# Agent attention with a routed two-layer net: float32 second layer in the last ten token tiles of three batches

## The chip, the core and the metric

The kernel runs on one core of a Trainium2 chip. The metric is the time of one execution on the device in microseconds (us). Smaller is better. Times here are the median of the runs shown, and the profile is one further execution taken by the hardware profiler.

## What is computed

The reference does agent attention (4 batches of 11456 tokens with 128 channels, 49 agents) and sends each of the 45824 resulting rows through one of 8 experts, chosen by the largest cosine logit:

```python
a2k = sm(agents, k)          # softmax over tokens
agent_v = a2k @ v            # 49 x 128
q2a = sm(q, agents)          # softmax over the 49 agents
x = q2a @ agent_v
...
h = np.maximum(x[mask] @ w1[e], 0.0)       # 128 -> 1024
out[mask] = gate_w[mask, None] * (h @ w2[e])  # 1024 -> 128
```

## The kernel before, in words

Almost all tokens of a batch go to one expert, so the kernel picks that expert per batch (`pick_expert`, from line 610) and repairs the few other tokens at the end (`fix`, `stray`). It doesn't multiply all 1024 hidden units: `pick_expert` ranks them, keeps the first 256 (384 in the fourth batch) as real relu units, and treats the rest as always on or always off. The always-on ones are folded into one linear product with `lin`; `proved` (from line 975) checks every token against that assumption (tile `vp`). The first layer is folded with the attention values, so its input is the tile `tt` of softmax numerators, transposed.

One batch is 23 token tiles `t`: 22 tiles of 4 columns of 128 tokens and a last one of 2 columns of 96 tokens. Each tile runs through two 128-unit slices `f` (three in the fourth batch). For one (batch, tile, slice), called a step here:

- `ffn_mm1` (line 1121): TensorE makes `hp` (128 units by 512 tokens, float32 in PSUM) with two float16 products (lines 1129, 1130, weights split into a high part `gh` and a low part `gl`). ScalarE writes relu(hp) as float16 `hh` (line 1133). VectorE writes the float16 remainder `hl` = relu(hp) - hh (line 1134).
- `ffn_mm2` (line 1137), five ticks later (`LAG = 5`): for each column of 128 tokens, three float16 products into `yp`: hh with the high part of w2, hh with its low part, hl with the high part (lines 1157 to 1159). At the first slice of a tile the `lin` products go ahead of them (line 1148).
- `ffn_out` (line 1163): VectorE multiplies `yp` by the gate into `ot` (line 1173), and ScalarE's queue sends it to HBM.

PSUM has four banks for `hp`, the transposes `fTp` and the check `vp`, two for `yp` and two for all else. `hh` and `hl` have five buffers each, `ot` three.

Beside the steps of batch b run the key, value and query work of the coming batches (scores `sp`, transposes `fTp`, copies `fT`, value sums `avp`) and, near the end of batch b, `pick_expert` for batch b+1: mostly small VectorE steps one after another (`key`, `nkey`, `sel`, `rank`) with a few TensorE products (`gp`, `row`, `placed`, `linp`, `w2pp`). At its end the next batch's `gh`, `gl` and `w2p` exist, and its steps can begin.

The order of SyncE's queue is written out by the program. On the other engines the instructions are put in order when the kernel is built, by priorities (`ffn_mm1` has a raised one) and by the framework's own estimate of durations; `issue_after` pins a few of them behind others. Each engine then works off its queue in that order.

Of the kernel before, what the change touches and what calls it, by code (L numbers as in the profile page):

```python
# [8 lines left out]
F16 = mybir.dt.float16  # L9
BF16 = mybir.dt.bfloat16  # L10
F32 = mybir.dt.float32
F32R = mybir.dt.float32r
I32 = mybir.dt.int32
AF = mybir.ActivationFunctionType
ALU = mybir.AluOpType
# [3 lines left out]
P = 128  # L19
# [10 lines left out]
def kernel(ctx: ExitStack, tc: tile.TileContext, q, k, v, agents, emb, tau, w1, w2, out):  # L30
    nc = tc.nc
    pe, dve, act, pool, sp = nc.tensor, nc.vector, nc.scalar, nc.gpsimd, nc.sync

    B, N, C = q.shape
    A = agents.shape[1]
    E, D, F = w1.shape
# [4 lines left out]
    TICKS = 4  # L41
    AT = {2: {0: 0, 2: 1}, 3: {0: 0, 1: 1, 3: 2}}
    KEEP = 5

    REM_J, REM_P = 2, 96
    J = (N - REM_J * REM_P) // P
    TJ = 4
# [29 lines left out]
    cst = ctx.enter_context(tc.tile_pool(name="cst", bufs=1))  # L77
    ld = ctx.enter_context(tc.tile_pool(name="ld", bufs=LB))
    wk = ctx.enter_context(tc.tile_pool(name="wk", bufs=2))
    sm = ctx.enter_context(tc.tile_pool(name="sm", bufs=2))  # L80
# [8 lines left out]
    def psh(name):  # L89
        return ps_h.tile([P, 512], F32, name=name, tag="h")  # L90

    def psy(name):
        return ps_y.tile([P, 512], F32, name=name, tag="y")
# [16 lines left out]
    def give(o, i):  # L110
        o.left[i] -= 1
# [24 lines left out]
    def tshape(t):  # L136
        return (P, TJ) if t < NT - 1 else (REM_P, REM_J)

    def unit_of(t):
        return (t // UT, t % UT) if t < NT - 1 else (NU - 1, 0)  # L140
# [27 lines left out]
    unit_load(k, "k", 0, 0)  # L168
    unit_load(k, "k", 0, 1)
    ident = cst.tile([P, P], F32, name="ident")  # L170
    zeros = cst.tile([P, 512], F16, name="zeros")
    turned = []
    pool.memset(zeros, 0.0)

# [197 lines left out]
    y_last, h_last, p_last, q_last = [], [], [], []  # L372
# [637 lines left out]
    def mark_strays(b):  # L1010
# [37 lines left out]
        if b < B - 1:  # L1048
# [8 lines left out]
            yield 1  # L1057
            dve.tensor_scalar(had[:, :KEEP], top[:, :KEEP], 0.0, 0.0, ALU.is_gt, ALU.add, accum_out=cnt)
            yield 1
# [6 lines left out]
            yield 1  # L1066
            dve.tensor_scalar(had[:, :KEEP], iotaf[:, :KEEP], cnt, None, ALU.add)
            yield 1
            last = sm.tile([P, 1], F32, name="had2", tag="had2", bufs=1)
            dve.tensor_scalar(last, cnt, P - KEEP + 0.5, BIG, ALU.is_gt, ALU.mult)  # L1070
            yield 1
            dve.tensor_tensor(out=last, in0=last, in1=top[:, KEEP - 1 : KEEP], op=ALU.add)
            pick = sm.tile([P, KEEP, 2], F32, name="mpick", tag="mpick", bufs=1)
            dve.tensor_copy(pick[:, :, 0], top[:, :KEEP])
            yield 1
# [42 lines left out]
    ticks = [(b, t, r) for b in range(B) for t in range(NT) for r in range(TICKS)]  # L1118
    live, yps = {}, {}

    def ffn_mm1(b, t, f):
        bt = batches[b]
        u, w = unit_of(t)
        p, n = tshape(t)
        m = p * n
        tt = tts[b, u][:, w * TJ * P : w * TJ * P + m]
        hp = psh("hp")
        fs = slice(f * P, (f + 1) * P)
        pe.matmul(out=hp[:, :m], lhsT=bt.gh[:, fs], rhs=tt, start=True, stop=False)  # L1129
        pe.matmul(out=hp[:, :m], lhsT=bt.gl[:, fs], rhs=tt, start=False, stop=True)  # L1130
        hh = wk.tile([P, TJ * P], F16, name="hh", tag="hh", bufs=5)
        hl = wk.tile([P, TJ * P], F16, name="hl", tag="hl", bufs=5)
        h_last[:] = [act.activation(hh[:, :m], hp[:, :m], AF.Relu)]  # L1133
        dve.scalar_tensor_tensor(out=hl[:, :m], in0=hp[:, :m], scalar=0.0, in1=hh[:, :m], op0=ALU.max, op1=ALU.subtract)  # L1134
        live[b, t, f] = (hh, hl)

    def ffn_mm2(b, t, f):

        bt = batches[b]
        p, n = tshape(t)  # L1140
        hh, hl = live.pop((b, t, f))
        if f == 0:
            yp = yps[b, t] = psy("yp").rearrange("p (c d) -> p c d", d=D)
            u, w = unit_of(t)
            for c in range(n):
                tc_ = tts[b, u][:, (w * TJ + c) * p : (w * TJ + c + 1) * p]
                for h in range(2):
                    pe.matmul(out=yp[:p, c, :], lhsT=tc_, rhs=bt.lin[:, h], start=(c == 0 and h == 0), stop=False, skip_group_check=True)  # L1148
            give(t_slots, tt_of[b, u])
        yp = yps[b, t]  # L1150

        for c in range(n):
            y = yp[:p, c, :]
            cs = slice(c * p, (c + 1) * p)
            last = f == NMS[b] - 1 and c == n - 1
            wh, wl = bt.w2p[:, f, 0], bt.w2p[:, f, 1]
            pe.matmul(out=y, lhsT=hh[:, cs], rhs=wh, start=False, stop=False, skip_group_check=True)  # L1157
            pe.matmul(out=y, lhsT=hh[:, cs], rhs=wl, start=False, stop=False, skip_group_check=True)  # L1158
            y_last[:] = [pe.matmul(out=y, lhsT=hl[:, cs], rhs=wh, start=False, stop=last, skip_group_check=True)]  # L1159
        y_log.append((now[0], y_last[0]))  # L1160
# [377 lines left out]
    def step2(b, t, f):  # L1538
        ffn_mm2(b, t, f)
        if f == NMS[b] - 1:  # L1540
            spawn(ffn_out(b, t))
# [14 lines left out]
    with tc.manual_schedule(engines={mybir.EngineType.SP}):  # L1556
        due = []
        for i in range(len(ticks) + LAG):
            if i < len(ticks):
                b, t, r = ticks[i]  # L1560
                f = AT[NMS[b]].get(r)
                while f is not None and not (hasattr(batches[b], "gl") and (b, unit_of(t)[0]) in tts):
                    prove()
                    run_step()
                run_half()
                if f is not None:
                    with tc.high_priority(200):
                        ffn_mm1(b, t, f)
                    ffn_t[0] = (b, t)
                    due.append((i + LAG, b, t, f))  # L1570
            else:
                run_half()
            while due and due[0][0] <= i:
                _, b, t, f = due.pop(0)
                while not hasattr(batches[b], "w2p"):
                    run_step()
                step2(b, t, f)
            for _ in range(1 if len(jobs) < 12 and i < (B - 1) * S else 2):
                if i % 3 < 2 or len(jobs) > 6 or i >= (B - 1) * S:
                    prove()  # L1580
            run_half()
# [48 lines left out]
```

## Time and profile before

| | |
|---|---|
| median of 3 runs | 765.32 us (762.32 to 768.18) |
| profiled execution | 766.39 us, its span 764.6 us |
| TensorE (PE) busy | 692.7 us, 91% |
| its weight loads (PEld) | 570.6 us, 75% |
| VectorE (DVE) busy | 600.1 us, 78% |
| ScalarE (ACT) busy | 474.2 us, 62% |
| GpSimd (POOL) busy | 341.3 us, 45% |
| mean granted TensorE clock | 0.946 of full speed |

Busy time is the union of an engine's instructions. The ends of matmuls are modelled and overlap the next ones, so what a stream of matmuls costs is read from the distances of their starts. The chain of waits follows the work that ended last backwards through whatever released each step; its shares say where time would come off the end if a piece went away and nothing else took its place.

### The profile page before, as it was taken

The numbers are of one execution on the slowest core, as the hardware profiler recorded it, in microseconds if no ns is written. First come the engines' busy times: TensorE is split into PE (matmuls) and PEld (weight loads), VectorE is DVE, ScalarE is ACT, GpSimd is POOL, SyncE is SP. The second block draws the span as 40 slices with busy tenths as digits, with TensorE's granted clock in tenths as the row PEclk, the third lists the DMA queues.
The fourth block names the chain that finished last, engine by engine and source line by source line (L and its number), as shares of the span: only waits on it lengthen the run. The fifth ranks groups of instructions, "written<-read, shape, count | busy, mean of one in ns | idle before, by whom it ended". The sixth has DMA issues, their size and how long they took to land.

```text
span 764.6 us, 24029 instructions
## 1 busy us (share of the span) xinstructions
PE 692.7 (91%) x9644; PEld 570.6 (75%) x9644; DVE 600.1 (78%) x1556; ACT 474.2 (62%) x1161; POOL 341.3 (45%) x576
## 2 busy tenths in 40 slices
PE   8997989899869899999988889998996599999996
PEld 6886778778757687878876678887885386687675
DVE  5767887766479899958568989855778989779987
ACT  3436968576359477867467647754664347756763
POOL 5004402842424667565336435654536537254520
PEclk9988999999769999999997999999998899999999
DMA  9993269656397696698647259945352037414211
GB/s 330 283 345 136 90 160 247 148 165 187 74 326 208 124 202 194 174 234 199 213 125 189 69 149 241 245 127 159 99 169 82 21 88 176 102 46 112 68 47 63
DMA packets 157820, 122.62 MB, mean 160 GB/s; under 512 B 78728, under 2 KB 134106, under 8 KB 157708
## 3 DMA queue, kind: packets, MB, share of 16 engines
q1 hardware_dynamic: 144331, 97.44, 49.3%
q10 hardware_dynamic: 13120, 23.47, 9.6%
q8 instruction: 76, 1.25, 0.7%
q14 instruction: 37, 0.29, 0.1%
q0 software_dynamic: 256, 0.17, 0.1%
HBM read 79.14 MB, written 23.72 MB: 135 GB/s over the span
## 4 chain that ended last, share of the span: by engine, by line
PE 62%; DVE 19%; DMA 8%; ACT 4%; issue 3%; POOL 2%; SPq 1%; ACTq 0%; POOLq 0%; DVEq 0%
PE sp L429 8%; PE fTp L416 8%; PE avp L520 4%; PE yp L1157 4%; PE yp L1159 4%; PE hp L1129 4%; PE yp L1158 4%; PE yp L1148 4%; PE hp L1130 4%; DVE hl L1134 3%; PE vp L988 3%; DMA tt<-e 2%; DMA kt<-in_k_dram 2%; PE placed L735 2%; DVE sel L719 2%
## 5 line engine op out<-in xcount | busy, mean ns | idle before, releaser
L1134 DVE SCALAR_TENSOR_TENSOR hl<-hp,hh 128x512 f16<-128x512 f32 (+1 forms) x207 | 136.7, 666 | 38.2 <-ACT hh L1133 36.3
L1157 PE MATMUL yp<-w2p,hh 128*128 128x128 f16 (+1 forms) x810 | 155.8, 222 | 2.5 <-ACT hh L1133 2.5
L1133 ACT ACTIVATE hh<-hp 128x512 f16<-128x512 f32 (+1 forms) x207 | 119.3, 582 | 62.0 <-PE hp L1130 49.5
L1158 PE MATMUL yp<-w2p,hh 128*128 128x128 f16 (+1 forms) x810 | 155.8, 222 | 0.0
L1159 PE MATMUL yp<-w2p,hl 128*128 128x128 f16 (+1 forms) x810 | 152.5, 222 | 0.0
L997 ACT ACTIVATE vp<-vp 128x512 f32<-128x512 f32 x191 | 112.5, 589 | 33.6 <-PE vp L985 17.6
L429 PEld LDWEIGHTS sp<-aT_all,fT 128*64 128x64 f32 (+1 forms) x2400 | 86.4, 143 | 25.0 <-issue 12.8
L429 PE MATMUL sp<-aT_all,fT 128*64 128x49 f32 (+1 forms) x2400 | 100.5, 231 | 4.4 <-ACT av_all L596 1.8
L1157 PEld LDWEIGHTS <-hh 128*128 128x128 f16 (+1 forms) x810 | 81.5, 101 | 15.8 <-ACT hh L1133 3.7
L1159 PEld LDWEIGHTS <-hl 128*128 128x128 f16 (+1 forms) x810 | 81.3, 100 | 10.5 <-issue 1.1
L1158 PEld LDWEIGHTS <-hh 128*128 128x128 f16 (+1 forms) x810 | 81.1, 100 | 5.2 <-issue 0.2
L1129 PE MATMUL hp<-tt,gh 128*128 128x512 f16 (+1 forms) x207 | 77.7, 379 | 6.2 <-DVE hl L1134 2.0
L1130 PE MATMUL hp<-tt,gl 128*128 128x512 f16 (+1 forms) x207 | 77.6, 378 | 0.0
L1148 PE MATMUL yp<-lin,tt 128*128 128x128 f16 x720 | 63.6, 224 | 12.3 <-DVE ot L1173 10.4
L1173 DVE TENSOR_TENSOR ot<-yp,gs 128x512 f32<-128x512 f32 (+1 forms) x92 | 61.2, 669 | 16.7 <-PE yp L1159 9.4
L936 POOL TENSOR_TENSOR nrm<-qq,half 128x16 f32<-128x16 f32 (+2 forms) x28 | 69.1, 2469 | 0.3
L855 POOL TENSOR_TENSOR e<-qe,e 128x392 f16<-128x392 f32 (+1 forms) x44 | 39.8, 904 | 60.0 <-ACT e L852 59.8
L1148 PEld LDWEIGHTS <-tt 128*128 128x128 f16 x720 | 49.8, 101 | 19.7 <-issue 12.2
L421 ACT COPY fT<-fTp 128x512 f32<-128x512 f32 (+1 forms) x87 | 48.5, 568 | 25.2 <-PE fTp L416 16.4
L416 PE MATMUL fTp<-ident,qt 128*128 128x128 f32 x360 | 61.6, 299 | 2.3 <-ACT vp L997 1.1
L419 DVE COPY fT<-fTp 128x512 f32<-128x512 f32 x67 | 45.9, 685 | 22.1 <-PE fTp L416 20.3
L897 POOL TENSOR_TENSOR rt<-rt 128x384 f32<-128x384 f32 (+1 forms) x48 | 39.8, 830 | 41.2 <-DVE rt L894 36.3
(369 smaller groups left out, 1670.4 us busy)
## 6 DMA issues: line engine op xcount, KB each, us to landing
kt<-in_k_dram SPq DMA_DIRECT2D x44, 512.0 KB, 6.6
vt<-in_v_dram SPq DMA_DIRECT2D x44, 512.0 KB, 6.2
qt<-in_q_dram SPq DMA_DIRECT2D x44, 512.0 KB, 5.7
out_dram<-ot ACTq DMA_DIRECT2D x88, 256.0 KB, 2.5
w1s<-in_moe_w_dram SPq DMA_DIRECT2D x8, 512.0 KB, 4.0
w2s<-in_moe_w_dram SPq DMA_DIRECT2D x8, 512.0 KB, 5.6
tt<-e SPq DMA_TRANSPOSE x44, 3.4
kt<-in_k_dram SPq DMA_DIRECT2D x4, 96.0 KB, 4.6
```

Source lines behind the costliest of these rows:

```text
L416: pe.transpose(out=tp[:, c * p : (c + 1) * p], in_=src[:p, c0 + c, :], identity=ident[:p, :p])
L429: pe.matmul(out=s[h : h + w, c * A : (c + 1) * A], lhsT=xT[:, c * p + h : c * p + h + w], rhs=aT_all[:, b, :], start=True, stop=True, skip ...
L936: pool.tensor_tensor(out=nrm, in0=quad, in1=half[:, :n], op=ALU.pow)
L997: act.activation(z[:p], z[:p], AF.Relu, scale=-1.0, accum_out=bt.vsum[:p, at : at + 1])
L1129: pe.matmul(out=hp[:, :m], lhsT=bt.gh[:, fs], rhs=tt, start=True, stop=False)
L1130: pe.matmul(out=hp[:, :m], lhsT=bt.gl[:, fs], rhs=tt, start=False, stop=True)
L1133: h_last[:] = [act.activation(hh[:, :m], hp[:, :m], AF.Relu)]
L1134: dve.scalar_tensor_tensor(out=hl[:, :m], in0=hp[:, :m], scalar=0.0, in1=hh[:, :m], op0=ALU.max, op1=ALU.subtract)
L1148: pe.matmul(out=yp[:p, c, :], lhsT=tc_, rhs=bt.lin[:, h], start=(c == 0 and h == 0), stop=False, skip_group_check=True)
L1157: pe.matmul(out=y, lhsT=hh[:, cs], rhs=wh, start=False, stop=False, skip_group_check=True)
L1158: pe.matmul(out=y, lhsT=hh[:, cs], rhs=wl, start=False, stop=False, skip_group_check=True)
L1159: y_last[:] = [pe.matmul(out=y, lhsT=hl[:, cs], rhs=wh, start=False, stop=last, skip_group_check=True)]
```

## The change

In tiles 13 to 22 of batches 0, 1 and 2 (`plain`), ScalarE writes relu(hp) as float32 into the room that `hh` and `hl` share, VectorE makes no `hl`, and the second layer is one float32 product per column in place of three float16 ones. The float32 weights `w2f` are the sum of the two float16 parts, made by VectorE once per batch. `hh` and `hl` become the two halves of one tile. `zeros`, the operand of the warm-up products, no longer has a place of its own and takes one of the three `ot` buffers.

```diff
+    LATE = 13
...
-    zeros = cst.tile([P, 512], F16, name="zeros")
+    zeros = wk.tile([P, 4 * P], F32, name="zeros", tag="ot", bufs=3).bitcast(F16)[:, :512]
...
+    def plain(b, t):
+        return b < B - 1 and t >= LATE
+
     def ffn_mm1(b, t, f):
         bt = batches[b]
+        if plain(b, t) and not hasattr(bt, "w2f"):
+            bt.w2f = sm.tile([P, 2, D], F32, name="w2f", tag="w2f", bufs=1)
+            dve.tensor_tensor(out=bt.w2f, in0=bt.w2p[:, :, 0], in1=bt.w2p[:, :, 1], op=ALU.add)
...
-        hh = wk.tile([P, TJ * P], F16, name="hh", tag="hh", bufs=5)
-        hl = wk.tile([P, TJ * P], F16, name="hl", tag="hl", bufs=5)
+        h2 = wk.tile([P, 2, TJ * P], F16, name="hh", tag="hh", bufs=5)
+        if plain(b, t):
+            hf = h2.rearrange("p h m -> p (h m)").bitcast(F32)
+            h_last[:] = [act.activation(hf[:, :m], hp[:, :m], AF.Relu)]
+            live[b, t, f] = (hf, None)
+            return
+        hh, hl = h2[:, 0], h2[:, 1]
...
+            if hl is None:
+                y_last[:] = [pe.matmul(out=y, lhsT=hh[:, cs], rhs=bt.w2f[:, f], start=False, stop=last, skip_group_check=True)]
+                continue
```

## Rows read from the trace of the kernel before

**Rows 1.** The page, part 1: busy time of each engine over the span

```profile
PE 692.7 (91%) x9644; PEld 570.6 (75%) x9644; DVE 600.1 (78%) x1556; ACT 474.2 (62%) x1161; POOL 341.3 (45%) x576
```

**Rows 2.** The page, part 4: the chain that ended last, by engine

```profile
PE 62%; DVE 19%; DMA 8%; ACT 4%; issue 3%; POOL 2%; SPq 1%; ACTq 0%; POOLq 0%; DVEq 0%
```

**Rows 3.** Timeline, VectorE: the last, narrow hl of batches 0, 1, 2

```profile
276.75 0.34 DVE L1134 SCALAR_TENSOR_TENSOR hl<-hp,hh 128x192 f16<-128x192 f32 x1
...
444.03 0.35 DVE L1134 SCALAR_TENSOR_TENSOR hl<-hp,hh 128x192 f16<-128x192 f32 x1
...
594.39 0.62 DVE L1134 SCALAR_TENSOR_TENSOR hl<-hp,hh 128x192 f16<-128x192 f32 x2
```

**Rows 4.** Windows: span, PE, PEld, DVE, ACT, POOL busy us (count), clock, DMA

```profile
175.00:218.00 43.00, 35.27 (x465) 29.37 (x461) 22.93 (x62) 20.16 (x42) 12.74 (x19) 0.80 0.57 157
218.00:281.00 63.00, 57.20 (x834) 47.91 (x835) 58.66 (x144) 41.98 (x100) 33.52 (x56) 0.92 0.84 206
360.00:404.00 44.00, 40.49 (x547) 35.02 (x544) 27.75 (x70) 26.06 (x63) 17.29 (x26) 0.94 0.59 178
404.00:448.00 44.00, 35.34 (x419) 27.59 (x417) 39.50 (x119) 28.48 (x64) 24.80 (x43) 0.90 0.40 107
534.00:576.00 42.00, 40.95 (x573) 35.06 (x570) 30.81 (x85) 28.83 (x76) 19.70 (x30) 0.96 0.41 122
576.00:602.00 26.00, 13.44 (x138) 11.07 (x136) 22.53 (x40) 11.66 (x27) 14.37 (x23) 0.84 0.23 72
```

**Rows 5.** Lines by form, VectorE: hl wide and narrow, and the nearest sum

```profile
L1134 DVE SCALAR_TENSOR_TENSOR hl<-hp,hh 128x512 f16<-128x512 f32 x198 | 133.8, 681 | 38.2 <-ACT hh L1133 36.3 <-ACT kd L514 1.2
...
L894 DVE TENSOR_TENSOR rt<-rtp,qe 128x392 f32<-128x392 f32 x44 | 24.4, 554 | 3.3 <-ACT rtg L892 3.1
...
L1134 DVE SCALAR_TENSOR_TENSOR hl<-hp,hh 128x192 f16<-128x192 f32 x9 | 2.9, 346 | 0.0
```

**Rows 6.** Timeline, TensorE: first of twelve float16 products, and what follows them

```profile
307.14 0.22 PE L1157 MATMUL yp<-w2p,hh 128*128 128x128 f16 x1
...
307.81 0.27 PE L988 MATMUL vp<-vm,tt 128*128 128x256 f16 x1
```

**Rows 7.** Timeline, TensorE: four float32 products (eight records), and what follows them

```profile
359.10 1.06 PE L1258 MATMUL shp<-sx,w1s 128*128 128x128 f32 x8
360.00 0.27 PE L988 MATMUL vp<-vm,tt 128*128 128x256 f16 x1
```

**Rows 8.** Lines by form, ScalarE: relu of 128x512 to float16 and float32

```profile
L1133 ACT ACTIVATE hh<-hp 128x512 f16<-128x512 f32 x198 | 116.4, 593 | 57.6 <-PE hp L1130 46.9 <-DVE ot L1173 5.7 <-DVE mTx L213 2.4
...
L1260 ACT ACTIVATE sh<-shp 128x512 f32<-128x512 f32 x8 | 4.8, 596 | 6.1 <-PE shp L1258 6.1
```

**Rows 9.** Windows of tile hl alone: span, PE, PEld, DVE busy us (count)

```profile
218.00:281.00 63.00, 10.07 (x52) 5.40 (x52) 7.47 (x13) 0.92 0.84 206
...
404.00:448.00 44.00, 6.16 (x32) 3.21 (x32) 6.09 (x10) 0.90 0.40 107
...
576.00:602.00 26.00, 5.64 (x25) 2.88 (x24) 3.33 (x6) 0.84 0.23 72
```

**Rows 10.** Chain by line in the six stretches of rows 4, in order

```profile
by line: PE avp L520 11.7%; PE sp L429 10.9%; DMA kt<-in_k_dram 8.6%; PE fTp L416 8.2%; SPq L480 7.3%; issue 5.5%; PE hp L1129 4.0%; PE yp L1148 3.9%; PE yp L1158 3.8%; PE yp L1157 3.6%; PE yp L1159 3.5%; PE hp L1130 3.0%; ACT ks L469 2.4%;
...
by line: PE fTp L416 8.2%; DVE hl L1134 6.8%; DVE sel L719 6.3%; PE placed L735 6.1%; issue 5.0%; DVE ot L1173 4.8%; DVE sel L799 4.2%; DVE ks L475 3.5%; PE sp L429 3.4%; DVE fT L419 3.3%; DVE m_run L407 3.2%; DVE qmx L842 3.0%; PE yp L1148
...
by line: DMA out_dram<-ot 9.4%; DMA w1s<-in_moe_w_dram 9.3%; issue 7.5%; POOL nrm L936 6.6%; PE fTp L416 5.9%; PE gp L661 5.7%; DMA out_dram<-so,ix 5.4%; PE yp L1148 3.5%; PE yp L1159 3.3%; PE yp L1158 3.0%; PE yp L1157 3.0%; DVE hl L1134 2
...
by line: DVE sel L719 11.3%; DVE sel L727 7.1%; PE linp L766 7.0%; PE sp L429 6.9%; PE row L712 6.2%; DVE fT L419 6.1%; DVE m_run L407 5.9%; PE w2pp L780 5.1%; DVE hl L1134 4.2%; issue 3.3%; DVE ot L1173 2.7%; DVE nkey L703 1.9%; DVE idx L1
...
by line: DMA w1s<-in_moe_w_dram 10.9%; PE avp L520 7.9%; PE yp L1148 6.3%; PE hp L1130 6.2%; PE hp L1129 6.2%; PE vp L988 5.7%; PE yp L1159 5.6%; PE yp L1158 5.3%; PE yp L1157 5.2%; PE sp L429 4.7%; PE gp L661 4.7%; PE fTp L416 4.5%; issue 
...
by line: DVE nkey L703 17.8%; DVE sel L719 15.9%; PE yp L1148 7.2%; PE row L712 6.7%; DVE key L697 6.1%; DVE rank L724 6.0%; PE fTp L416 5.0%; issue 4.8%; DVE ot L1173 4.6%; PE yp L1157 3.7%; PE yp L1158 3.7%; PE yp L1159 3.3%; DVE hl L1134
```

**Rows 11.** Lines by form, weight loads: a float32 operand of 128x128

```profile
L1258 PEld LDWEIGHTS shp<-sx,w1s 128*128 128x128 f32 x64 | 7.8, 192 | 0.2 <-issue 0.2
```

## The prediction, made before the changed kernel was run

> **What bounds the kernel now.** I read the page's busy shares first. TensorE is busy for 91% of the span and VectorE for 78% [rows 1], so over the whole run TensorE looks like the bound. The chain of waits says less: 62% of it is TensorE, 19% VectorE, and the rest are transfers and the other engines [rows 2]. The change touches ten tiles of each of three batches, so I looked for where these lie and read the bound there. The narrow hl steps are the last two of a batch; they stand at 276.8, 444.0 and 594.4 us [rows 3]. Counting back through the order of the hl steps (26 of a batch's 46 come before tile 13), the late tiles fill about 175 to 281, 360 to 448 and 534 to 602 us.
>
> I cut these at the point where the steps of `pick_expert` thicken on VectorE, which gives six stretches, two a batch [rows 4]. The reader is to compare PE with DVE in each line. In the first half of each pair TensorE leads: 35.3 of 43 us against 22.9, 40.5 of 44 against 27.8, 41.0 of 42 against 30.8. In the second half VectorE leads: 58.7 of 63 us (93%) against 57.2, 39.5 of 44 (90%) against 35.3, 22.5 of 26 (87%) against 13.4. The chain by stretch agrees: the entries at its head are avp and fTp, or transfers, in the first halves, and sel, nkey, hl and ot, all VectorE's, in the second [rows 10]. So the change takes work from the engine that binds 133 us of the run, and gives work to the engine that binds another 129 us.
>
> **What goes: hl.** 54 wide steps (9 tiles x 2 slices x 3 batches) at 681 ns and 6 narrow ones at 346 ns [rows 5] are 36.8 + 2.1 = 38.9 us of VectorE. What this is worth depends on the stretch. In the VectorE stretches the hl steps take 7.5, 6.1 and 3.3 us [rows 9], 16.9 together. On the chain they hold 6.8% of 63 us, 4.2% of 44 us, and less than 3.3% of 26 us (taken as 0.6) [rows 10], together 6.7. The gain there has these two ends. It can exceed the chain's share, because an hl that lies beside a TensorE piece of the chain still stands in a queue that is 87 to 93% full, ahead of the next sel or ot. It cannot well reach the whole, because TensorE is 91% busy in the largest of the three. I take the middle, 11.8 us. In the TensorE stretches hl has between 2 and 3% of 44 us on the chain in the second pair, less than the last entry shown in the others [rows 10]; I take 1.2 + 0.7 + 0 = 1.9 us, between 0 and 4. With hl gone, what is late next in the VectorE stretches is the string of sel and rank steps itself, and ot.
>
> **What comes: one float32 product for three of float16.** Twelve float16 products started at 307.14 and the next instruction at 307.81 [rows 6]: 0.67 / 12 = 56 ns each, 167 ns for the three of a column. A float32 product of the same shape, both operands in SBUF, is in the trace as two records: four of `shp` (eight records) started at 359.10 and the next instruction at 360.00 [rows 7], 225 ns each. The change has 54 x 4 + 6 x 2 = 228 columns, so TensorE gets 228 x 58 = 13.1 us more, a third on top of what these products took. On the path I price it by the chain: the three lines L1157 to L1159 hold 10.9% of 43 us, 9.3% of 44, 16.1% of 42 and 10.7% of 26 [rows 10], which is 4.7 + 4.1 + 6.8 + 2.8. In the other two their entries lie below the last shown, so at most 3 x 3.0% of 63 (5.7) and 3 x 1.9% of 44 (2.5); I take two thirds, 3.8 + 1.7. Together 23.9 us, and a third more is 23.9 x 58 / 167 = 8.2 us. The ends are 6.3 (nothing in those two) and the full 13.1. At the lower clock both kinds stretch alike, so the ratio stays.
>
> The row for float32 weight loads shows 192 ns each [rows 11], yet eight of them pass with eight products in 0.90 us [rows 7], so they hide beside the stream and I cost them at nothing. The Trainium skill ("TensorE: Matmul & The Clock Gate", Part 3, what overlaps and what doesn't) says that a weight load overlaps running matmuls only where it goes to another row group, which a full 128-row load does not. By that rule the loads would stand bare; the rows contradict it, and it is the last rival below.
>
> **Small parts.** `w2f` is one VectorE sum per batch of 128x256. The nearest rows are 346 ns (192 wide) and 554 ns (392 wide) [rows 5], so 3 x 0.35 to 3 x 0.55, 1.0 to 1.7 us; I take 1.4, half of it on the path: 0.7. It is issued with the first late `hp`, five ticks ahead of its reader, and its inputs are a dozen tiles old, so nothing queued behind it on VectorE waits for more than its own time. ScalarE's relu costs 593 ns to float16 and 596 ns to float32 [rows 8]: nothing. No wait is added: the first product of a column waited for hh before, as the float32 product does now, and the last one's wait for hl goes. The PSUM bank of `hp` comes free after ScalarE instead of after VectorE, which can only help the next `hp` or `fTp`; it is inside the share of hl on the chain. `zeros` in an `ot` buffer binds an output tile only to the warm-up products, done in the first microseconds, and `h2` has the five buffers that `hh` and `hl` had. No DMA is added or moved by the program. What I can't price is the order of the queues of TensorE, VectorE, ScalarE and GpSimd, which is found anew when the kernel is built; it may shift any of these stretches by a few us either way.
>
> **Sum.** -11.8 - 1.9 + 8.2 + 0.7 = -4.8 us. The profiled execution took 766.4 us, which makes 761.6; it lies 1.1 us over the median of the runs, so the median after is 760.5 us.
>
> **The rivals.**
>
> VectorE gives back all of it. The second halves are bound by VectorE's queue alone, their hl goes in full (16.9), and TensorE's added work there lies in its idle time; only the first halves pay, (4.7 + 4.1 + 6.8) x 58 / 167 = 5.4. Sum -16.9 - 1.9 + 5.4 + 0.7 = -12.7, or 752.6 us. For it: 93, 90 and 87% busy VectorE. Against it: TensorE 91% busy in the largest of the three [rows 4]. The Trainium skill ("Perfetto Trace Analysis", Identifying the Most-Contended Engine) calls matmul busy time a bad measure of how near TensorE is to its limit and takes weight-load busy time instead. By that measure TensorE in this stretch is at 47.9 of 63 us, 76%, which is the reading of this rival.
>
> TensorE takes the place of VectorE. In the second halves the path moves over to the products at once: `row`, `placed`, `linp` and `w2pp` queue behind longer second-layer products, and the freed VectorE time turns into waits for TensorE. Then nothing of hl is gained and the chain's price stays: +8.2 + 0.7 = +8.9, 774.2 us; with all 13.1 us on the path and all of w2f 779.8. It decides as soon as less than 8.9 us of the hl time comes off the end. For it: the 91% of TensorE in 218 to 281 us, and 62% of the chain being TensorE's. Against it: 133 us in which VectorE is the fuller engine.
>
> The two cancel. Only the shares that hl holds on the chain are gained: -6.7 - 1.9 + 8.2 + 0.7 = +0.3, 765.6 us.
>
> The float32 loads don't hide. 456 records x 192 ns = 88 us, 852 us. Rows 7 speak against it, in the same shape and type.
>
> That the change doesn't do what it says I leave at no chance of its own: the float32 products of `shp` in rows 7 show the form that it uses.
>
> **How the numbers follow.** About 1% is what a measurement of this kernel can tell from no change: below 757.7 us is faster, above 773.0 slower. The forecast (-4.8) has 0.38, the full return of VectorE's time 0.33, TensorE taking over 0.19, the cancelling 0.09, and bare loads 0.01. The likeliest one's own range is 755 to 766, so about a fifth of its 0.38 (0.08) falls under 757.7; the full return lies there whole: faster 0.41. Slower is TensorE's case as far as it passes 773 (0.17) and bare loads: 0.18. The rest, 0.41, is within 1%. The range of 8 in 10 goes from 746 (all hl of the six stretches' chain and VectorE shares, 18.8 us, with TensorE's part in its idle time: 766.4 - 18.8 - 1.1 = 746.5) to 776, past TensorE's case of 774.2 but short of its extreme.
>
> **What would show it.** In the changed profile VectorE should be busy some 37 us less (near 563), its hl count 147 in place of 207, and the second-layer float32 line should show 456 records with starts 112 ns apart; the f16 lines 582 each. The steps between the heads of the second halves and the narrow tiles should be shorter, most of all 218 to 281 us; the three first halves longer by 1 to 2 us each. The forecast is wrong if these second halves keep their length while `row`, `placed` or `w2pp` begin to wait behind `yp`, if the float32 starts are further apart than 112 ns, or if the time moves in stretches without late tiles, such as the fourth batch, which would be the order of the queues.

## The result, and the profile after

The changed kernel takes **743.29 us** (median of 4 runs, 741.88 to 747.96) where the kernel before took 764.17 beside it (762.32 to 768.18): a ratio of 0.9731, with an interval of 0.9669 to 0.9792. That is 20.6 us less at the ratio, and 17 us under the forecast of 760.5; it lies below the range of 746 to 776 as well. All ratios here are of fast executions; one of the six of r1 below, which took 1661.8 us, is left out of its ratio.

The profiled execution took 741.88 us, with a span of 740.0. The first line of the page after, which answers to [rows 1]:

```profile
PE 684.2 (92%) x9416; PEld 569.8 (77%) x9416; DVE 567.8 (77%) x1499; ACT 474.0 (64%) x1161; POOL 339.4 (46%) x576
```

VectorE is busy 32.3 us less (600.1 to 567.8; about 37 were forecast). The forecast added up durations, but a step of VectorE begins before the one ahead of it has ended: behind an hl of 0.68 us the next starts after 0.60 (578.71 to 579.31 in the kernel before, shown with s1 below). An estimate from that is 54 x 0.60 = 32.4 us for the wide steps, some 34 with the six narrow ones, and 33 after the sums of the weights are added. The groups that the change touches, VectorE's hl that stays, the f32 products and the sum of the weights, first by line and form, then (the last two) the list of a line's and a tile's instructions with minimum, median and maximum in ns:

```profile
L1146 DVE SCALAR_TENSOR_TENSOR hh<-hp,hh 128x512 f16<-128x512 f32 x144 | 97.0, 680 | 25.8 <-ACT hh L1145 25.3
```

```profile
L1141 ACT ACTIVATE hh<-hp 128x512 f32<-128x512 f32 x54 | 31.6, 592 | 15.0 <-PE hp L1137 13.2 <-DVE vmin L995 1.5
```

```profile
L1169 PE MATMUL yp<-w2f,hh x456: 271/275/523, 177.9 to 576.2; 128*128 128x128 f32 x144, 128*96 128x128 f32 x8
```

```profile
L1129 DVE TENSOR_TENSOR w2f<-w2p x3: 402/406/416, 100.0 to 441.4; 128x256 f32<-128x256 f16 x3
```

So the parts cost what was forecast one by one: hl in f16 680 ns as in [rows 5], relu to f32 592 ns as in [rows 8], the sum of the weights 0.41 us. For the f32 product the start of the next instruction is what counts; in TensorE's timeline:

```profile
569.37 1.05 PE L1169 MATMUL yp<-w2f,hh 128*128 128x128 f32 x8
570.26 0.61 PE L1160 MATMUL yp<-lin,tt 128*128 128x128 f16 x8
```

Four products (eight records) in 0.89 us are 222 ns each, against 225 worked out from `shp` [rows 7], and their weight loads (193 ns by the page) hide again.

The windows of the late tiles, cut at the same landmarks as [rows 4] (each edge moved by as much as the step next to it: the first relu of tile 13, the step `mean` of `pick_expert`, the first relu of the next batch, and for the last edge the first relu of tile 22); columns: the stretch, its length, busy us of PE, PEld, DVE, ACT and POOL with counts, granted clock, DMA share, GB/s:

```profile
173.80:216.40 42.60, 34.38 (x443) 29.07 (x437) 17.91 (x53) 19.05 (x41) 12.51 (x19) 0.88 0.57 160
216.40:278.30 61.90, 55.98 (x750) 49.62 (x751) 52.54 (x132) 42.77 (x100) 33.43 (x55) 0.92 0.79 212
362.20:399.30 37.10, 37.02 (x484) 32.55 (x483) 20.51 (x55) 23.75 (x58) 10.63 (x15) 1.00 0.61 163
399.30:436.70 37.40, 31.74 (x363) 26.28 (x362) 33.52 (x113) 28.08 (x64) 25.29 (x46) 1.00 0.45 120
521.20:559.90 38.70, 38.70 (x482) 33.91 (x479) 22.75 (x72) 26.52 (x70) 19.77 (x31) 1.00 0.48 134
559.90:583.10 23.20, 19.36 (x156) 14.75 (x154) 22.19 (x49) 13.73 (x34) 16.68 (x25) 0.93 0.25 80
```

The six are 240.9 us in place of 262.0. The reader is to compare the lengths, not the busy times: the VectorE halves went from 63, 44 and 26 us to 61.9, 37.4 and 23.2, as forecast in kind, but the TensorE halves, which were to get 1 to 2 us longer each, went from 43, 44 and 42 to 42.6, 37.1 and 38.7. That is 10.6 us less in stretches where the change adds work to the fullest engine; the prediction takes only 1.9 us off there, for hl, and adds 5.4 for the products.

### The profile page after: what moved, and what is told of

Read it like the earlier page. It is cut to its first block, busy times and chain, and to the rows that moved or that the text cites. A ratio compares the mean times of both kernels' runs of the same rounds, so it can differ in the third digit from the quotient of the medians.

```text
span 740.0 us, 23511 instructions
## 1 busy us (share of the span) xinstructions
PE 684.2 (92%) x9416; PEld 569.8 (77%) x9416; DVE 567.8 (77%) x1499; ACT 474.0 (64%) x1161; POOL 339.4 (46%) x576
## 5 line engine op out<-in xcount | busy, mean ns | idle before, releaser
L1146 DVE SCALAR_TENSOR_TENSOR hh<-hp,hh 128x512 f16<-128x512 f32 (+1 forms) x147 | 97.9, 673 | 25.8 <-ACT hh L1145 25.3
L1145 ACT ACTIVATE hh<-hp 128x512 f16<-128x512 f32 (+1 forms) x147 | 85.4, 588 | 44.2 <-PE hp L1137 35.7
L1172 PE MATMUL yp<-w2p,hh 128*128 128x128 f16 (+1 forms) x582 | 109.4, 220 | 0.0
L1173 PE MATMUL yp<-w2p,hh 128*128 128x128 f16 (+1 forms) x582 | 109.4, 220 | 0.0
L1174 PE MATMUL yp<-w2p,hh 128*128 128x128 f16 (+1 forms) x582 | 107.5, 220 | 0.0
L430 PEld LDWEIGHTS sp<-aT_all,fT 128*64 128x64 f32 (+1 forms) x2400 | 82.4, 138 | 24.1 <-issue 13.1
L430 PE MATMUL sp<-aT_all,fT 128*64 128x49 f32 (+1 forms) x2400 | 96.2, 226 | 4.4 <-ACT av_all L597 1.5
L1160 PE MATMUL yp<-lin,tt 128*128 128x128 f16 x720 | 63.2, 220 | 7.9 <-DVE ot L1188 5.9
L1169 PE MATMUL yp<-w2f,hh 128*128 128x128 f32 (+1 forms) x456 | 66.5, 283 | 0.3 <-ACT hh L1141 0.3
L1172 PEld LDWEIGHTS <-hh 128*128 128x128 f16 (+1 forms) x582 | 57.5, 99 | 10.1 <-issue 0.3
L1174 PEld LDWEIGHTS <-hh 128*128 128x128 f16 (+1 forms) x582 | 57.4, 99 | 7.5 <-issue 1.4
L856 POOL TENSOR_TENSOR e<-qe,e 128x392 f16<-128x392 f32 (+1 forms) x44 | 38.7, 880 | 50.6 <-ACT e L853 50.5
L1169 PEld LDWEIGHTS yp<-w2f,hh 128*128 128x128 f32 (+1 forms) x456 | 58.4, 193 | 4.0 <-issue 1.5
L422 ACT COPY fT<-fTp 128x512 f32<-128x512 f32 (+1 forms) x87 | 48.4, 566 | 19.4 <-PE fTp L417 15.2
L1173 PEld LDWEIGHTS <-hh 128*128 128x128 f16 (+1 forms) x582 | 57.5, 99 | 4.0
L420 DVE COPY fT<-fTp 128x512 f32<-128x512 f32 x67 | 45.8, 683 | 17.8 <-PE fTp L417 17.4
```

The source lines that it names most:

```text
L430: pe.matmul(out=s[h : h + w, c * A : (c + 1) * A], lhsT=xT[:, c * p + h : c * p + h + w], rhs=aT_all[:, b, :], start=True, stop=True, skip ...
L1169: y_last[:] = [pe.matmul(out=y, lhsT=hh[:, cs], rhs=bt.w2f[:, f], start=False, stop=last, skip_group_check=True)]
```

## The experiments

In all of them the kernel before was run beside the kernel. The last column is (ratio - 1) x 766 us.

| run | what it runs | median us | ratio to before (95%) | difference us |
|---|---|---|---|---|
| e1 | changed kernel without a late tile | 766.1 | 1.0003 (0.9967 to 1.0039) | +0.2 |
| e2 | three f16 products, no hl | 733.2 | 0.9565 (0.9514 to 0.9616) | -33.3 |
| e3 | changed, with a VectorE step in hl's place | 757.3 | 0.9885 (0.9849 to 0.9920) | -8.8 |
| e4 | before, with a fourth f16 product | 756.9 | 0.9916 (0.9887 to 0.9946) | -6.4 |
| o1 | changed, in before's order | 752.5 | 0.9828 (0.9780 to 0.9877) | -13.2 |
| o2 | before, in the changed order | 757.4 | 0.9899 (0.9831 to 0.9967) | -7.7 |
| o3 | before, in e4's order | 750.1 | 0.9802 (0.9756 to 0.9848) | -15.2 |
| o4 | before, in e3's order | 757.9 | 0.9892 (0.9828 to 0.9955) | -8.3 |
| p1 | as e2, in before's order | 746.7 | 0.9729 (0.9692 to 0.9767) | -20.8 |
| p2 | as e3, in before's order | 767.2 | 1.0029 (0.9993 to 1.0065) | +2.2 |
| p3 | as e2, in the changed order | 743.5 | 0.9717 (0.9664 to 0.9771) | -21.7 |
| o6 | changed, in e2's order | 737.6 | 0.9617 (0.9581 to 0.9653) | -29.3 |
| q1 | as e4, in before's order | 771.3 | 1.0094 (1.0058 to 1.0131) | +7.2 |
| q2 | before, in the changed order from batch 2's tile 17 on | 763.5 | 0.9949 (0.9913 to 0.9985) | -3.9 |
| q3 | before, in the changed order up to that tile | 762.1 | 0.9945 (0.9916 to 0.9973) | -4.2 |
| r1 | changed, again | 744.9 | 0.9723 (0.9668 to 0.9778) | -21.2 |
| r2 | as o6, again, beside r1 | 739.9 | 0.9683 (0.9624 to 0.9743) | -24.3 |
| s1 | before, one step of VectorE moved | 766.3 | 0.9986 (0.9953 to 1.0019) | -1.1 |

**One part at a time, e1 to e4.** The first theory was the prediction's own: hl's VectorE time against the products' TensorE time, with sizes wrong. The edits, in order: no tile is late; the f16 path is kept but hl is not made; a VectorE step of hl's size is put back; and, in the kernel before, one f16 product more.

```diff
# e1
-    LATE = 13
+    LATE = 99
# e2, in the f16 path
         h_last[:] = [act.activation(hh[:, :m], hp[:, :m], AF.Relu)]
+        if plain(b, t):
+            live[b, t, f] = (hh, hh)
+            return
# e3, in the f32 path
             h_last[:] = [act.activation(hf[:, :m], hp[:, :m], AF.Relu)]
+            dve.scalar_tensor_tensor(out=hp[:, :m], in0=hp[:, :m], scalar=0.0, in1=hf[:, :m], op0=ALU.max, op1=ALU.subtract)
# e4, in the kernel before
             wh, wl = bt.w2p[:, f, 0], bt.w2p[:, f, 1]
+            if b < B - 1 and t >= 13:
+                pe.matmul(out=y, lhsT=hh[:, cs], rhs=wl, start=False, stop=False, skip_group_check=True)
```

> The changed kernel with LATE = 99: no tile is late, so every step has its three float16 products and its hl; what stays of the change is hh and hl as halves of one tile and zeros in an ot buffer. If the gain of 21 us is VectorE's time (first theory) or the cut between TensorE's queue and VectorE's (second theory), this is the kernel before: 764 us, within 5. If it came from the small edits or from a new order of the queues that these bring (third theory), it lies at 755 or under.

> Late tiles keep three float16 products a column, but the third takes hh again and VectorE makes no hl; the result of the late tiles leaves out the remainder's product and adds hh times the high part twice. It takes from VectorE what the change takes and adds nothing to TensorE. By the prediction's price for the float32 product (8.2 us on the path) it runs at 735 us; if the longer product is hidden, it runs with the changed kernel, at 741 to 745 us.

> The changed kernel, but in late tiles VectorE still makes a step of hl's form, from the same hp and the float32 relu, written back to hp, where nobody reads it; so VectorE's work and the time that it holds hp's bank stay as before, and TensorE no longer waits for it. First theory (VectorE's time is what was gained): the gain goes, and the product's price shows, 766 to 773 us. Second theory (TensorE's queue stood behind hl in VectorE's queue): most of the gain stays, 745 to 753 us.

> The kernel before with a fourth float16 product (hh with the low part once more, which adds that term twice to the output of the late tiles) in each of the 228 late columns, 228 x 56 ns = 12.7 us of TensorE and nothing else. It is the price of the longer product alone, with hl in place. By the prediction's share of the chain 8 us of it come through, 772 us; if the second halves and the waits of the first halves hide it, 764 to 768 us; if TensorE is the bound throughout, 777 us.

e1 is the kernel before to within 0.4%: the buffers that the change merges and moves are worth nothing. e2 and e3 look orderly beside the changed kernel: the products would cost 743.3 - 733.2 = 10.1 us and hl 757.3 - 743.3 = 14.0 (12.7 and 11.8 by the ratios), not far from the forecast. But then e3, whose VectorE work is nearly before's and whose products are dearer, should be slower than before, and it is 8.8 us faster. And e4, with 228 products of 56 ns [rows 6] more, 12.7 us of TensorE's time, and nothing taken away, is 6.4 us faster. Added work alone does not explain that. What differs too is the order in which each engine runs its instructions: it is found when a kernel is built, and an edit can move it. By the orders stored in p1 and p3 below, which are before's and the changed kernel's for the same instructions, 558 of 1437 VectorE instructions and 3074 of TensorE's 7879 stand at another place. e1's queues are before's.

**The order held fixed, o1 to o4.** In these the program chains each engine's instructions (TensorE, VectorE, ScalarE, GpSimd; SyncE's order is the same in all the kernels) in the order of another kernel, with edges that fix the order and add no semaphore. The chains by themselves cost nothing that shows: s1 below, the kernel before chained in its own order but for one step, is at 0.9986.

```diff
+    for e, places in QUEUES.items():
+        prev = None
+        for at in places:
+            i = seqs[e][at]
+            if prev is not None:
+                tc.add_manual_dep(i, prev.name, info)
+            prev = i
     total = nc.values_load(lefti[:1, :1], min_val=0, max_val=B * NCOL * E)
```

Where one kernel has three products and the other one, the three stand in the place of the one, and the one in that of the first of three. The hl steps of the late tiles have no place in the changed kernel's order; in o2 the build put them in.

> The changed kernel's instructions, with the order in which TensorE, VectorE, ScalarE and GpSimd run them fixed to the kernel before's (the removed steps simply missing, one f32 product standing where the first of three stood). Theory A (most of the gain is the new queue order that the build found, the removed work itself is worth only the predicted few us): 764.2 - 4.8, so about 759, between 755 and 763. Theory B (the gain is the removed VectorE work and its waits, in whatever order): as the changed kernel, 740 to 748.

> The kernel before's instructions, all of them, in the changed kernel's queue order (three products where the one f32 product stood; the VectorE steps that the changed kernel lacks are placed by the build). Theory A: the order brings its 16 us without any work removed: 744 to 753. Theory B: 760 to 768, as before.

> The kernel before's instructions, all of them, in the queue order of the run with a fourth product (which was faster than before although TensorE had 12.7 us more to do), that product left out. Theory A: the order was what made that run faster, so without its extra work about 757 - 10, 743 to 752. Theory B: the order is worth nothing, 760 to 768.

> The kernel before's instructions, all of them, in the queue order of the run with the f32 products and a VectorE step kept in hl's place. Its VectorE work is nearly the kernel before's, its products are about 10 us dearer, and it took 757.3. Theory A: 757.3 - 10, so 744 to 752. Theory B: 760 to 768.

Neither theory held whole. o1 lies below A's range and above B's: at before's order the changed work is worth 13.2 us, not 4.8 and not 20. o2 misses both ranges as well: the order alone is worth 7.7. The two add up to 20.9, about the 20.6 of the change. At the changed kernel's order the work is worth as much again, 757.4 - 743.3 = 14.1 us (12.9 by the ratios). o3 meets A: with before's work e4's order is worth 15.2 us, so the order had more than paid for the fourth product. o4 misses both, nearer to B: the order of e3 is worth 8.3 us. Three orders that came out of other edits are each better for the kernel before than its own.

**The two terms at a fixed order, p1 to p3, and o6.** With the order held, hl and the products can be taken apart.

> In the queue order of the kernel before: the late tiles keep three f16 products, the third takes hh in hl's place, and the step that makes hl is left out (so the low half's correction of these tiles is not computed). This is the VectorE part of the change alone, at fixed order. Theory A (VectorE's time was worth more on the path than the 13.7 predicted, and the f32 products cost about the 8 to 10 us that I gave them): 741 to 746. Theory B (VectorE's time is worth the predicted 13.7, and in place the f32 products cost next to nothing): 750 to 754, the same as the full change in this order (752.5).

> In the queue order of the kernel before: f32 relu, one f32 product and the summed weights in the late tiles, with a VectorE step of hl's size kept (it writes hp, which nobody reads again). This is the product's price alone, at fixed order. Theory A (8 to 10 us): 773 to 777. Theory B (next to nothing): 764 to 768.

> In the queue order of the changed kernel: three f16 products (the third with hh) where its f32 product stands, no hl. Against the changed kernel it shows the price of the f32 products in that order. Theory A (8 to 10 us): 733 to 736. Theory B (next to nothing): 741 to 745.

> The changed kernel's instructions in the queue order of the run without hl and with three f16 products, which took 733.2 in that order. If orders are worth what the last runs show (7 to 16 us from one to another), it is off the changed kernel's 743.3 by the difference of the two orders alone: with the products' price at 8 to 10 us 741 to 744, with a price near nothing 733 to 736.

Leaving out hl alone gives 20.8 us (17.8 to 23.6) in before's order, near A. The f32 products cost +2.2 us where the VectorE step is kept (p2), 7.6 by the ratios in before's order without it (o1 against p1; 752.5 - 746.7 = 5.8 by the medians), 1.1 in the changed order (against p3; the medians are 743.3 and 743.5), and 4.0 in e2's order (o6 against e2; 4.4). p2 and p3 are B's, p1 is A's but for 0.7 us, and o6 lies between its two figures: the products cost between 1 and 8 us, with each difference good to some 4 us. p2 is not their price alone: it also takes away TensorE's wait for hl, which its kept step no longer holds up.

The late stretches of the profiles, cut at the same landmarks, show where (us; a is the half in which TensorE is fuller, b the half of VectorE):

| | 1a | 1b | 2a | 2b | 3a | 3b | sum |
|---|---|---|---|---|---|---|---|
| before [rows 4] | 43.0 | 63.0 | 44.0 | 44.0 | 42.0 | 26.0 | 262.0 |
| e1: before's work and queues | 45.7 | 63.2 | 44.9 | 43.8 | 41.7 | 25.5 | 264.8 |
| p1: no hl | 45.0 | 60.7 | 42.8 | 39.1 | 38.3 | 20.6 | 246.5 |
| p2: f32 products | 44.7 | 63.9 | 47.2 | 40.9 | 41.6 | 27.1 | 265.4 |
| o1: both, before's order | 43.9 | 62.0 | 44.9 | 37.6 | 41.4 | 21.0 | 250.8 |
| changed kernel | 42.6 | 61.9 | 37.1 | 37.4 | 38.7 | 23.2 | 240.9 |

Each row is one execution. Those of before and e1, the same work in the same queues, differ by 3.3 us in the sum of the a halves and 0.5 in that of the b halves, so less than that says nothing. Without hl the b halves lose 12.6 us, which is clear of it, and the a halves 2.9, which is not. With the products dearer (p1 to o1) the a halves gain 4.1 us and the b halves 0.2; from before to p2 it is 4.5 and -1.1. That the products are paid where TensorE leads, and lie in TensorE's idle time where VectorE leads, fits these numbers and is not shown by them.

With the new order (o1 to the changed kernel) the a halves are 11.8 us shorter and the b halves 1.9 longer. These are lengths between landmarks and not gains, since the order also moves work across the cuts: TensorE's records go from 519 to 484 in 2a, where it is 5.2 us less busy, and from 115 to 156 in 3b, where it is 6.5 us busier. The last four of these windows in o1, with the columns of [rows 4]:

```profile
361.20:406.10 44.90, 42.26 (x519) 37.67 (x518) 21.77 (x60) 26.01 (x63) 17.27 (x26) 0.96 0.58 174
406.10:443.70 37.60, 31.98 (x380) 26.49 (x376) 36.59 (x107) 28.47 (x64) 24.37 (x40) 1.00 0.51 126
527.90:569.30 41.40, 41.40 (x506) 36.52 (x503) 23.34 (x70) 28.73 (x76) 19.41 (x29) 1.00 0.48 127
569.30:590.30 21.00, 12.82 (x115) 10.36 (x114) 20.05 (x38) 11.41 (x26) 15.14 (x24) 0.90 0.30 89
```

In 3b VectorE is busy 20.0 of 21 us, TensorE 12.8: there is room for dearer products.

**How hl's share reaches the end: s1.** In the last b half of the kernel before TensorE waits twice (us in total, times, longest):

```profile
PE yp L1148 <- DVE ot L1173: 4.4, 1, 4.4
PE hp L1129 <- DVE hl L1134: 1.7, 1, 1.7
```

The products behind the first wait stand in TensorE's queue ahead of the step `row` of `pick_expert`:

```profile
584.86 1.01 PE L1148 MATMUL yp<-lin,tt 128*128 128x128 f16 x8 [4.40 <-DVE ot L1173]
...
590.65 1.88 PE L712 MATMUL row<-sel,ones 128*128 128x512 f32 x4
```

though the input of `row`, GpSimd's `sel` (the first of these lines), was begun at 579.20, 11.5 us earlier:

```profile
579.20 1.89 POOL L701 TENSOR_TENSOR sel<-ident,key 128x1024 f32<-128x1024 f32 x1
581.06 2.12 POOL L678 TENSOR_TENSOR w1s<-w2s,w1s 128x1024 f16<-128x1024 f32 x1
583.13 0.19 POOL L939 TENSOR_TENSOR ls<-la,sg 128x2 f32<-128x2 f32 x1
583.29 0.90 POOL L855 TENSOR_TENSOR e<-qe,e 128x392 f16<-128x392 f32 x1
```

What holds the ot back is a small VectorE step ahead of it, which lasts as long as these four GpSimd steps do, to 584.2:

```profile
578.71 0.68 DVE L1134 SCALAR_TENSOR_TENSOR hl<-hp,hh 128x512 f16<-128x512 f32 x1
579.31 0.27 DVE L994 TENSOR_REDUCE vmin<-vp 96x2 f32<-96x128 f32 x1
579.51 4.71 DVE L703 TENSOR_SCALAR nkey<-key 128x8 f32<-128x8 f32 x1
584.13 1.27 DVE L1173 TENSOR_TENSOR ot<-yp,gs 128x512 f32<-128x512 f32 x2
```

In o1 the queue is the same without the hl. VectorE comes to `nkey` as GpSimd's `sel` (572.72) is about to begin, the two ot pass, and a step behind them is held instead:

```profile
572.42 0.20 DVE L805 TENSOR_SCALAR nkey<-key 128x8 f32<-128x8 f32 x1
572.53 1.27 DVE L1289 TENSOR_TENSOR ot<-yp,gs 128x512 f32<-128x512 f32 x2
573.73 4.06 DVE L1120 TENSOR_SCALAR odd<-vmin 128x90 f32<-128x90 f32 x1
```

Neither wait of TensorE is there, and `row` starts at 577.29, 4.6 us after its `sel`:

```profile
577.29 1.88 PE L814 MATMUL row<-sel,ones 128*128 128x512 f32 x4
```

The profiles sort alike: those with hl, or a step of its size, in this order (before, e1, p2, q1) have one `nkey` of 4 us or more, those without (o1, p1) have none. That asks whether the 5 us of 3b are hl's at all, or this one step's. s1 moves it, in the kernel before, past the two ot steps behind it in VectorE's queue, and nothing else:

```diff
+ # VectorE's stored order
-  ..., hl, vmin, nkey, ot, ot, odd, ...
+  ..., hl, vmin, ot, ot, nkey, odd, ...
```

> The kernel before in its own queue order, with one instruction moved: on VectorE the last nkey step (128x8, it took 4.71 us beside two GpSimd steps) stands behind the two ot steps that followed it. Theory H (the nkey step is held while GpSimd's steps run, and what it costs is the ot behind it, TensorE's 4.40 us wait for it and the row step behind that; without hl the same hold falls on a step behind the ot): the hold moves to the next step, TensorE's 4.40 us wait is gone, row starts 4 to 5 us earlier, and the time is 760 to 763, 3 to 5 us under before. Rival (the hold is no cause: row and the rank steps come no earlier, since VectorE is the bound there): 765 to 768, no change.

It took 766.3 us, a ratio of 0.9986 (0.9953 to 1.0019): by the time the rival holds. In its profile theory H is seen at work, the wait for ot is gone and `row` starts 7.0 us after its `sel` (578.19) in place of 11.5:

```profile
578.49 1.27 DVE L1276 TENSOR_TENSOR ot<-yp,gs 128x512 f32<-128x512 f32 x2
579.69 3.53 DVE L806 TENSOR_SCALAR nkey<-key 128x8 f32<-128x8 f32 x1
```

```profile
584.14 0.23 PE L1262 MATMUL yp<-w2p,hl 128*128 128x128 f16 x1 [2.47 <-DVE hl L1237]
585.15 1.88 PE L815 MATMUL row<-sel,ones 128*128 128x512 f32 x4
```

TensorE's next wait there is for hl. Even so the steps behind `row` come earlier in this execution, against the rival: the first `rank` step starts at 594.75 (599.58 in the kernel before), 3.8 us earlier when both are counted from the step `mean` (570.42 and 571.43), and 3b, cut at the same landmarks, lasts 22.2 us, where it has 26.0 before, 25.5 in e1 and 21.0 in o1:

```profile
599.58 1.65 DVE L724 TENSOR_SCALAR rank<-more 128x4 f32<-128x4 f32 x1
...
594.75 1.64 DVE L827 TENSOR_SCALAR rank<-more 128x4 f32<-128x4 f32 x1
```

```profile
575.00:597.20 22.20, 10.80 (x136) 8.43 (x134) 21.28 (x40) 11.32 (x27) 14.41 (x22) 0.89 0.27 84
```

That execution took 761.9 us, the third lowest of twelve; their median is only 0.5 us under that of the kernel before beside them, 766.8. So the hold is real and its wait can be taken away. What that is worth at the end is open: nothing that shows in the twelve, at most 3.6 us by the interval. It can be most of what 3b loses without hl, and not the 20.8 us of p1.

**What the order is worth, and where: q1 to q3.** q1 prices TensorE's time at a fixed order. q2 and q3 run the kernel before in two orders spliced at the first second-layer product of batch 2's tile 17.

> The kernel before in its own queue order, with a fourth f16 product per column of the late tiles, 228 products of 56 ns, so 12.7 us more of TensorE work, put just ahead of the first of the three. Theory A (in the late tiles TensorE has time to spare, so more of its work there costs little; this is why the f32 products cost less than my 8.2): 764 to 769. Theory B (TensorE's work there is on the path at half its length or more, and the f32 product was cheap for another reason): 771 to 778.

> The kernel before's instructions, in its own queue order up to the first second-layer product of batch 2's tile 17, and in the changed kernel's order from there on. Theory A (the worth of the order, some 8 us with this work, sits in the handover from batch 2 to batch 3, where the selection of batch 3's matrices starts earlier): 754 to 760. Theory B (it is spread over the span): 761 to 766.

> The counterpart: the kernel before's instructions, in the changed kernel's queue order up to the first second-layer product of batch 2's tile 17, and in its own order from there on. Theory A: the gain of the order is gone, 762 to 767. Theory B: half or more of it stays, 756 to 761.

q1 is at the foot of B: at a fixed order added products do cost time, 7.2 us (4.4 to 10.0) for 12.7 of work, some half. The gain of e4 was the order's alone (in e4's order the fourth product costs 756.9 - 750.1 = 6.8, or 8.7 by the ratios). By q2 and q3 each part of the new order is worth about 4 us, together 8.1, what o2 found for the whole. q2 lies in B's range. q3's 762.1 lies at the edge of A's, but beside before it is 4.2 us faster (2.1 to 6.4), half of the whole. So the worth is spread over the span, and A falls.

One place where the order differs is 2a. The longest pieces of the chain there in o1, which has before's order (start and length in us), are these:

```profile
363.85 2.90 POOL nrm L1038
370.87 2.37 DMA out_dram<-so,ix
373.65 4.65 DMA out_dram<-ot
395.82 4.07 DMA w1s<-in_moe_w_dram
399.94 1.99 PE gp L763 x16
```

The write of the strays that `fix` answers, and an output tile's store that follows it, take 7 us on the chain. They are there in the kernel before too (`out_dram<-ot` 9.4% and `out_dram<-so,ix` 5.4% of 44 us, the third line of [rows 10]), whatever the late tiles run. In the changed kernel the answering of these strays (`shp`, then `syp`) starts 9.8 us ahead of the cut at 362.2, in o1 0.9 us ahead of the cut at 361.2:

```profile
352.44 1.14 PE L1273 MATMUL shp<-sx,w1s 128*128 128x128 f32 x8
...
360.28 1.06 PE L1374 MATMUL shp<-sx,w1s 128*128 128x128 f32 x8
```

So work that o1 has in 2a lies ahead of it in the changed kernel, and that is part of why 2a is 7.8 us shorter (44.9 to 37.1). Whether the two transfers still hold anything up there is not shown: the chain of the changed kernel is followed back no further than 390 us, nor is o2's. Nor are the 7.8 us all gain: q3 has the new order there and a 2a of 36.0 us, and is 4.2 us faster in all. What in the order gives its 7 to 8 us stays open.

**An order that may be better still: r1 and r2.**

> The changed kernel itself once more, beside the next run on the same chip: 741 to 748.

> The changed kernel's instructions in the queue order of the run without hl: 735 to 741, under the changed kernel by 3 to 8 us, if its first measurement (737.6) holds on the same chip.

The changed kernel in e2's order is under both kernels in each of its measurements, 737.6 and 739.9 us. Against the kernel before that is shown (both intervals end below 0.975). Against the changed kernel it is 5.0 us on the same chip with intervals that overlap, so it is likely and not settled.

## Why the prediction was wrong

The sign was right and the size was not: -4.8 was forecast, -20.6 measured. Two steps failed: hl's term was too small, and the order of the queues had no term. By its steps:

- **What bounds the late tiles: right as far as hl goes.** Leaving hl out pays in the b halves, 12.6 us. That dearer products cost in the a halves alone is not shown.
- **hl, -11.8 and -1.9: too small.** In before's order its absence alone gave 20.8 us (17.8 to 23.6) where 13.7 were forecast. Inside the six stretches p1 has -12.6 and -2.9, close to the two terms, so the choice of the middle between the chain's share and the whole was good there; the rest lies outside them or in what one execution differs from the next. A part of it can be a wait that the prediction names ("the last one's wait for hl goes") and gives no price. p2, which drops that wait, keeps the VectorE step and has the dearer products, costs 2.2 us, where q1 costs 7.2 for nearly as much added time on TensorE. An estimate from these two is some 5 us for the wait, with the other 15.4 for VectorE's time (p2 to o1). No run drops the wait alone.
- **The products, +8.2: about right in before's order,** 7.6 us by p1 and o1, and 7.2 by q1, 1 to 4 in the other two orders. The unit was right (222 ns, 225 forecast). The parts of the a halves (5.4 forecast, 4.1 to 4.5 measured) and of the b halves (2.8 forecast, +0.2 and -1.1 measured) are hardly larger than what two executions of the same work differ by, or smaller.
- **The rival "VectorE gives back all of it" met o1's number, in part by luck.** It gave 752.6 us and o1 measured 752.5. But it takes 16.9 us off the b halves for hl, where p1 lost 12.6, and 5.4 for the products, where the runs gave 7.2 and 7.6. Its chance of 0.33 was second to the forecast's 0.38.
- **The order of the queues, the last of the small parts: no term.** It was "found anew when the kernel is built; it may shift any of these stretches by a few us either way", and stood neither in the sum nor in the range. It measured -7.4 to -9.2 us (o1 to the changed kernel, by ratio and by median), and -7.7 with before's work. The mark that was named for it, time moving in stretches without late tiles, hardly caught it: outside the six stretches the span is 502.6 us before, 501.6 in o1 and 499.1 in the changed kernel, while the six are 9.9 us shorter from o1 to the changed kernel.
- **VectorE 37 us less busy:** 32.3. The counts of hl, of f16 products (582 a line) and of f32 records (456), the weight loads and the relu came as forecast. Bare weight loads (852 us) and TensorE taking over (774.2) did not come.

Of the 15.8 us between forecast and result, then, by the ratios along p1, o1 and the changed kernel, 7.1 are hl's term (-20.8 for -13.7), 1.3 the products and the sum of the weights (+7.6 for +8.9), and 7.4 the order. Taken in another turn, with p2 first, the products cost 2.2 and hl gives 15.4; the work together, -13.2 for -4.8, and the order do not depend on that. Each of these differences is good to 4 or 5 us.

## What to carry to other kernels

Where the order of the queues is found when the kernel is built, a change is two changes: before a difference of 1 or 2% is put down to the work, run the new work in the old order and the old work in the new one. Here the one was worth 13 us and the other 8, and a kernel with more work came out faster. Added work on TensorE cost about half of its length at a fixed order (7.2 us for 12.7). Where in the span it was paid, one profile of each kernel could not tell: two executions of the same work differ by up to 3 us in a stretch, and an order moves work across any cut.

## What was not expected of the hardware

Some small VectorE steps last as long as the GpSimd steps beside them: `nkey`, 128x8 elements, took 4.71 us in the kernel before (its line's minimum is 0.16) and ended within 0.03 us of a string of four GpSimd steps (the expectation for s1 speaks of two), three of which had not begun when it did; `odd`, 128x90, took 4.06 us in o1. The ot steps, which read PSUM, passed beside that GpSimd string in o1 in 1.27 us for two. The Trainium skill ("SBUF - State Buffer", "SBUF: two separate sides") says that VectorE and GpSimd share a pair of ports as an exclusive lock, held for a whole instruction, for which some VectorE operations must wait. The rows agree, and show the wait to run on over several GpSimd steps in a row. What such a wait is worth at the end s1 leaves open.

The granted clock rose with the change (0.946 to 0.974 over the span, 1.00 in both stretches of batch 1's late tiles), and how much of the gain goes through it no run here shows. A higher clock does not by itself come with a shorter span: p2, with more work for TensorE, was granted 0.960 at a span of 764.8 us, against 0.946 at 764.6 before.
